# Transposing one more attention output by DMA instead of on TensorE, in a fused attention and MLP kernel

## The chip, the cores and the metric

The kernel runs on one core of one Trainium2 chip. The metric is device time in microseconds (us) of one execution; lower is better.

## The reference

Sliding-window attention with a few global keys and a distance bias, followed by an MLP with squared ReLU. The shapes are batch 4, 8 heads, 768 positions and head size 64; `n_global` is 8 and `n_local` is 96. In the MLP there are 3072 tokens, a model width of 512 and an inner width of 2048.

```python
scores = scale * np.matmul(q, k.transpose(0, 1, 3, 2))
...
keep = is_global | is_local
...
scores = np.where(keep, scores + bias, -1000000000.0)
a = np.exp(scores - np.max(scores, axis=-1, keepdims=True))
a = a / (np.sum(a, axis=-1, keepdims=True) + 1e-09)
x = np.matmul(a, v)                      # then to (tokens, heads * head size)
h = x @ w_in
r = np.maximum(h, 0.0)
out = (r * r) @ w_out
```

## The kernel before

The 3072 tokens are cut into 24 tiles of 128, six for each batch element. The MLP works on blocks of two tiles, so there are 12 blocks. Block 3, which matters here, consists of tiles 6 and 7.

**Attention of one tile j.** GpSimd issues the loads of q, k and v (line 213). From tile 6 on, q and k land in a ring of three slots, so the load of tile j waits until tile j-3 has been read. q and k are transposed into `qkT`. Tiles 0 to 5 do that on TensorE (`tr`, line 402), and the others by one DMA transpose on SyncE's queue (`T`, line 426). TensorE makes the scores of the tile with itself and with its left neighbour (`sc`, line 489, 16 matmuls, or 8 for the first tile of a batch element). These contract over 64 rows only. ScalarE takes the exponential (`exp`, line 555), VectorE multiplies by the bias and mask (`mul`, line 580), TensorE multiplies by v (`pv`, line 642, two groups of 8 matmuls into `po`), and VectorE divides by the row sum into `x` (`norm`, lines 669 and 670).

**From x to the MLP.** The MLP needs x with the model width on the partitions. There are two ways, chosen by `j < JX` in line 698. Tiles below JX are transposed on TensorE by four matmuls with the identity into a PSUM buffer (`trx`, line 705), which ScalarE or VectorE then copies to `xT` (line 332, or 330). The other tiles use one DMA transpose on SyncE's queue (`xT`, line 729), and nothing else. `JX` is 8.

**MLP of one block.** A block has eight steps. `s1` (line 757) is eight matmuls of 256 columns; it needs `xT` of both tiles of its block. ScalarE takes the ReLU (line 778) and VectorE squares it (line 790). `s2` (line 830) is four matmuls of 512 columns into two accumulators. After the eighth step the result is copied out (`o`) and stored from SyncE's queue (`st`, line 872). Up to 14 squared tiles `hs` can wait for their `s2`. In the text below, s1 steps are numbered through: step 24 is the first of block 3.

**Order.** Each engine executes its instructions in one fixed order, written out before the kernel runs. A small planner (class `Plan`) makes it: it gives every operation a duration, a set of operations it depends on and a rank (`key`), and always takes the operation with the smallest start plus 0.01 times its rank. So 100 points of rank stand for 1 us. The tables around the change only move ranks and dependencies. `SHIFT` adds to the rank of a kind of operation, or of that kind in one tile. `LEADS` moves all the attention of a tile ahead of its block's MLP steps. `STEP` names the s1 step after which a tile's scores may come, and `HOLD` makes the following s1 step wait for those scores. A gate (line 376), which is a tiny write on VectorE, delays the loads of tiles 8 to 10, since the load has to come after it.

For a DMA transpose of x the planner counts 1.2 us on SyncE's queue, and 0.9 us of transfer with two lags of 0.6 and 1.2 us; for some tiles more is added by `SAFEX` (tiles 9, 11 and 13). The transposes of q and k have such additions for tiles 6 to 11 and 14 to 16 in `SAFE`.

Of the kernel before, what the change touches and what calls it, by code (L numbers as in the profile page):

```python
# [21 lines left out]
class Plan:  # L22
# [8 lines left out]

    LAG = {"PE": 0.25, "ACT": 0.26, "DVE": 0.2, "SP": 0.6, "POOLQ": 0.8, "DMAQ": 1.2, "DMA": 0.0}
    URGE = 0.01
    SHIFT = {'T': 47, 'sc': -5.25, 'pv': -2, 'norm': 26.5, 'trx': -2, 'xT': 51, 'gk': 42, 'gv': -127.5, 'mul': 24, 'kl': 38.5, 'relu': 25.5, 'sq': 30, 's2': -5, 'o': 61, 'st': 78, ('mul', 3): 28, ('tr', 4): 10, ('xT', 5): -22, ('sc', 6): 14, ('pv', 7): -4, ('norm', 7): -17, ('trx', 7): -3, ('sc', 8): -12, ('pv', 8): -18, ('pv', 10): 45, ('sc', 11): 12, ('pv', 12): -50, ('sc', 13): 17, ('sc', 14): 6, ('pv', 14): 10, ('norm', 14): -28, ('sc', 15): -21, ('exp', 15): 20, ('exp', 16): 83, ('mul', 16): 92, ('norm', 16): -9, ('sc', 17): 32, ('pv', 17): 28, ('pv', 21): 9.5, ('pv', 22): -10, ('norm', 22): 8, ('s1', 2): -8.5, ('sq', 2): -10, ('relu', 3): 24, ('sq', 3): -82, ('s1', 5): 6, ('s1', 6): 30, ('sq', 6): 6, ('s1', 7): -6, ('sq', 7): -92, ('relu', 8): 40, ('s1', 9): -2, ('s1', 10): -10, ('s2', 0): 7.5, ('s2', 2): 1, ('s2', 4): -15, ('s2', 5): 37, ('s2', 6): -5, ('s2', 7): -3, ('s2', 9): 4.5, ('s2', 11): 30}

    def shift(self, name):
        early = name[-1 if name[0] in ("T", "tr") else 1]
        return self.SHIFT.get(name[0], 0.0) + self.SHIFT.get((name[0], early), 0.0)

# [65 lines left out]
def kernel(  # L105
# [35 lines left out]
    NFIRST = 4  # L141
    NSPLIT = 4
    NBIAS = 3
    JQK, JX = 6, 8
    NQ, NKT = 3, 2 * TPB
    NG = 8 - NACC
    G = ("g", NG)
# [7 lines left out]
    def const(shape, dt, name):  # L155
        return consts.tile(shape, dt, name=name, tag=name)
# [18 lines left out]
    pbt = const([P, 2, P], FP32, "pbt")  # L175
    pbw = const([P, 2, P], FP32, "pbw")
    plan = Plan()
    LEADS = {3: 51, 4: 17, 5: 16, 6: 27, 8: 2, 9: 20, 10: 42, 11: 47, 12: 0, 14: 0, 15: 7.5, 16: 34, 17: 46, 20: 28, 21: 15, 23: 56}
    SAFE = {j: 1.6 for j in range(6, 12)} | {14: 4.2, 15: 3.2, 16: 3.5}
    SAFEX = {9: 1.5, 11: 1.5, 13: 2.5}  # L180

# [2 lines left out]
    JOIN = {(7, 0), (12, 0), (21, 0), (16, 0), (23, 0), (18, 0), (20, 0), (15, 0)}  # L184
    COPY = [14, 15, 19, 20, 22]
    BEHIND = {}
    HOLD = ((10, 0),)
    STEP = {(4, 0): -7, (12, 0): 37, (5, 0): -2, (10, 0): 29, (13, 0): 30, (23, 1): 81}
    JGATE = 11
    NHS = 14  # L190
    NWARM = 8
# [12 lines left out]
    def slot(j):  # L204

        return j if j < NFIRST + 2 else NFIRST + 2 + j % NQ
# [57 lines left out]
    def emit_ones(e, js):  # L264
        for j in js:
            nc.vector.memset(v_sb[j][:, :, D : D + 1], 1.0)
# [38 lines left out]
    for g in range(NFIRST + 2, NT, 6):  # L305
        js = range(g, min(g + 6, NT))
        o = plan.op(
            ("ones", g), {"DVE": 0.2}, lambda e, js=js: emit_ones(e, js),
            key=-1.0, ready=15.0,
        )  # L310
# [40 lines left out]
    kl = [const([P, NPAIR, P], BF16, f"kl_{i}") for i in range(2 if COPY else 0)]  # L351
# [8 lines left out]
    for j in range(NT):  # L360
        b, t = divmod(j, TPB)
        first = t == 0
        need = 8 * (j // 2)
        base = need - LEADS.get(j, LEAD) + 4 * (j % 2)
        if (j, 0) in JOIN:
# [3 lines left out]
        if j in late:  # L369
            def emit_load(e, j=j):  # L370
                load_tile(j)
            gate = None
            if NFIRST + 2 + NQ - 1 <= j < JGATE:

                def emit_gate(e, j=j):
                    nc.vector.memset(qk_ring[slot(j)][:, :, :1], 0.0)

                gate = plan.op(
                    ("gate", j), {"DVE": 0.07}, emit_gate, deps=qk_users[slot(j)] + [ld, xT_sp.get(j - 3)],
                    key=base - 9,  # L380
                )
# [13 lines left out]
        for n in range(2) if j < JQK else ():  # L395
            users = []

            def emit_tr(e, j=j, n=n, fp=fp):
# [9 lines left out]
            tr = plan.op(  # L408
                ("tr", n, j), {"PE": 0.5 if fp else 0.24}, emit_tr,
                deps=[land["qk"[n], j]], key=base, takes=(*G, [users]),  # L410
            )
# [12 lines left out]
        if j >= JQK:  # L424
            def emit_dT(e, j=j, T_=T_):
# [5 lines left out]
            T = plan.op(  # L431
                ("T", j), {"SP": 1.3}, emit_dT,
                deps=[land["q", j], land["k", j], xT_op[j - 3]] + ku, key=base - 6,
            )
            T = plan.op(("moved", j), {"DMAQ": 1.2}, None, deps=[T])
            qk_users[slot(j)].append(T)
            if j in SAFE:

                T = plan.op(("seen", j), {"DMA": SAFE[j]}, None, deps=[T])
# [6 lines left out]
        mul, mul_users = {}, {}  # L446
# [55 lines left out]
        for gs in SETS.get(j, [tuple(range(groups))]):  # L502
            n = 8 * len(gs)
            sc_users = busers[2 * gs[0] : 2 * gs[-1] + 2]
            if (j, gs[0]) in JOIN:

                o, also, taken = joint
# [16 lines left out]
            if j < NBIAS:  # L524
# [6 lines left out]
            o = plan.op(  # L531
                ("sc", j, gs[0]), {"PE": 0.2 + 0.029 * n},
                lambda e, gs=also, f=emit_sc: f(e, gs), deps=[*deps, bias],
                key=base + 1 + 2 * gs[0], takes=takes,
            )
# [91 lines left out]
        norm = []  # L627
# [170 lines left out]
    for o in plan.ops:  # L798
        if o["name"][0] == "sc":
            j = o["name"][1]  # L800
            n = STEP.get(o["name"][1:], 4 * j - LEAD)
            if n >= 0 and j >= NFIRST:
                o["deps"].append(s1_ops[n // NSTEP, n % NSTEP])
                if o["name"][1:] in HOLD:
                    n += 1
                    s1_ops[n // NSTEP, n % NSTEP]["deps"].append(o)

    for blk in range(NBLK):
# [9 lines left out]
        for s, sub, half in order2:  # L818
# [5 lines left out]
            def emit_s2(e, blk=blk, s=s, sub=sub, half=half, w=w, cols=cols, own=own):  # L824
# [15 lines left out]
            o = plan.op(  # L840
                ("s2", blk, s, sub), {"PE": 0.43 * w / d_model}, emit_s2,
                deps=[d, land["wout", s]] + users[-1:],
                key=8 * blk + s + 2.0 + (0 if not last else 8 * sub + 8 * (half or 0)),
                takes=((*G, [users]) if own else ("acc", NACC, [users])) if s == 0 else None,
            )
# [6 lines left out]
            if s == NSTEP - 1:  # L852
# [14 lines left out]
                def emit_st(e, blk=blk, sub=sub, half=half, cols=cols):  # L867
# [9 lines left out]
                st = plan.op(  # L877
                    ("st", blk, sub), {"SP": 0.8 if (blk, sub) in HALVES else 0.4}, emit_st,
                    deps=[ev, s1_ops[NLATE, 0] if blk < NLATE - 2 else None],
                    key=8 * blk + s + 9.0,  # L880
                )
                st = plan.op(("stored", blk, sub), {"DMAQ": 1.4}, None, deps=[st])
# [40 lines left out]
```

## Time and profile before

| | before |
|---|---|
| median of 5 runs | 211.81 us (211.33 to 212.38) |
| the profiled execution: its own time | 211.69 us |
| its span in the profile | 209.9 us |
| TensorE matmuls, busy | 202.5 us (96% of the span) |
| VectorE / ScalarE busy | 141.0 us / 120.2 us |
| `trx` transposes on TensorE | 32, four for each of tiles 0 to 7 |
| DMA transposes of x / of q and k | 16 / 18 |

The span is what the profile covers, from the first to the last instruction of the kernel; the execution's own time is 1.8 us longer. "Busy" for matmuls counts overlapping instructions once, and a matmul's recorded duration includes the time in which the next has already started, so the distance between the starts of two matmuls tells more than their durations. A few matmul records are missing from a trace. Of the 400 `s2` matmuls, 373 have one.

### The profile page before, as it was taken

Reading aid. Unit: us, or ns where it says so; the run is one execution under the profiler, and the core shown is the slowest. Engines: PE = TensorE matmul, PEld = TensorE weight load, DVE = VectorE, ACT = ScalarE, POOL = GpSimd, SP = SyncE. Lnnn points to the kernel's source line nnn. Section 1 sums busy time; section 2 is a strip of 40 time slices with the busy share of each in tenths; the row PEclk is TensorE's granted clock in tenths of the full one; section 3 lists DMA queues with packets and bytes.
Section 4 is the critical chain, followed back from the end, with each engine's and each line's share of the span. In section 5 each row is a group of like instructions: output and inputs, shape, how many; then the busy total and the mean of one; then the engine's idle time right before and its main releaser. Section 6 shows DMA issues by size and latency. Waiting matters only on the chain.

```text
span 209.9 us, 4980 instructions
## 1 busy us (share of the span) xinstructions
PE 202.5 (96%) x1957; PEld 141.3 (67%) x1984; DVE 141.0 (67%) x370; ACT 120.2 (57%) x224; POOL 73.9 (35%) x91
## 2 busy tenths in 40 slices
PE   7988999999999999999999999999999999999994
PEld 3766877666756677676866676776676865865853
DVE  7689698533595878585958666676696865781730
ACT  6766678234772674664737464663575826841631
POOL 8996676531568048232455143222500000000000
PEclk9999999999999999999999999999999999999999
DMA  9999999999999999979999994989983421130402
GB/s 128 153 160 185 182 190 200 179 162 142 211 132 163 201 120 158 192 119 134 175 146 108 217 97 58 139 120 144 195 61 75 123 55 28 53 97 3 102 0 100
DMA packets 112649, 27.32 MB, mean 130 GB/s; under 512 B 103282, under 2 KB 109682, under 8 KB 112626
## 3 DMA queue, kind: packets, MB, share of 16 engines
q0 software_dynamic: 79200, 13.37, 83.8%
q1 hardware_dynamic: 33426, 13.64, 35.6%
q8 instruction: 15, 0.25, 0.5%
q14 instruction: 8, 0.07, 0.1%
HBM read 27.26 MB, written 6.29 MB: 160 GB/s over the span
## 4 chain that ended last, share of the span: by engine, by line
PE 88%; POOL 5%; DMA 4%; issue 1%; DVE 1%; ACT 0%; POOLq 0%
PE acc L830 39%; PE hT L757 39%; PE sc L489 5%; PE po L642 4%; DMA win<-in_moe_w_in_dram 4%; POOL qk L213 3%; POOL v L213 2%; POOL win L213 1%; PE trx L705 1%; PE tr L402 1%; DVE x L670 0%; DVE hs L790 0%; POOL pbi L269 0%; DVE rs L669 0%; ACT o L330 0%
## 5 line engine op out<-in xcount | busy, mean ns | idle before, releaser
L757 PE MATMUL hT<-xT,win 128*128 128x256 bf16 x768 | 93.5, 273 | 0.8 <-DMA win<-in_moe_w_in_dram 0.8
L830 PE MATMUL acc<-wout,hs 128*128 128x512 bf16 (+2 forms) x373 | 87.1, 370 | 1.7 <-issue 0.3
L778 ACT ACTIVATE hr<-hT 128x512 f32<-128x512 f32 x96 | 57.4, 603 | 47.4 <-PE hT L757 41.8
L757 PEld LDWEIGHTS <-win 128*128 128x128 bf16 x768 | 72.6, 97 | 15.3 <-DMA win<-in_moe_w_in_dram 1.4
L790 DVE TENSOR_TENSOR hs<-hr 128x512 bf16<-128x512 f32 x96 | 64.7, 686 | 23.2 <-ACT hr L778 22.4
L830 PEld LDWEIGHTS <-hs 128*128 128x128 bf16 x400 | 36.7, 97 | 33.9
L555 ACT ACTIVATE esc<-sc 128x512 bf16<-128x512 f32 x78 | 39.9, 613 | 13.2 <-PE sc L489 13.2
L213 POOL DMA_DIRECT2D qk<-in_q_dram x23 | 20.8, 903 | 69.7 <-DMA qkT<-qk 57.4
L580 DVE TENSOR_TENSOR at<-esc,E 128x512 bf16<-128x512 bf16 x78 | 32.3, 422 | 10.0 <-ACT esc L555 7.2
L330 ACT COPY o<-acc 128x512 f32<-128x512 f32 (+2 forms) x21 | 11.6, 576 | 19.8 <-PE acc L830 19.8
L213 POOL DMA_DIRECT2D v<-in_v_dram x24 | 21.9, 914 | 1.4 <-DMA win<-in_moe_w_in_dram 1.1
L670 DVE TENSOR_TENSOR x<-po,rs 128x256 bf16<-128x256 f32 x48 | 20.4, 424 | 1.7
L213 POOL DMA_DIRECT2D qk<-in_k_dram x23 | 20.7, 902 | 0.6 <-DMA win<-in_moe_w_in_dram 0.5
L642 PEld LDWEIGHTS <-at 128*128 128x128 bf16 x352 | 15.6, 97 | 5.5 <-ACT at L555 0.9
L642 PE MATMUL po<-v,at 128*128 128x65 bf16 x352 | 17.3, 194 | 0.7 <-DMA v<-in_v_dram 0.7
L669 DVE RECIPROCAL rs<-po 128x4 f32<-128x4 f32 x48 | 8.5, 177 | 11.8 <-PE po L642 11.4
L489 PEld LDWEIGHTS <-qkT 64*128 64x128 bf16 x312 | 9.4, 94 | 5.6 <-issue 4.9
L489 PE MATMUL sc<-qkT 64*128 64x128 bf16 x192 | 12.5, 219 | 0.0
L489 PE MATMUL sc<-qkT,qkT 64*128 64x128 bf16 x120 | 8.5, 216 | 0.0
L332 DVE COPY o<-acc 128x512 f32<-128x512 f32 x4 | 2.8, 692 | 6.2 <-PE acc L830 6.2
L213 POOL DMA_DIRECT2D win<-in_moe_w_in_dram x8 | 6.2, 804 | 1.6 <-DMA win<-in_moe_w_in_dram 1.2
L213 POOL DMA_DIRECT2D wout<-in_moe_w_out_dram x8 | 5.7, 718 | 2.3 <-DMA win<-in_moe_w_in_dram 1.6
(45 smaller groups left out, 68.7 us busy)
## 6 DMA issues: line engine op xcount, KB each, us to landing
out_dram<-o SPq DMA_DIRECT2D x21, 256.0 KB, 3.5
v<-in_v_dram POOLq DMA_DIRECT2D x24, 128.0 KB, 5.9
qk<-in_q_dram POOLq DMA_DIRECT2D x23, 128.0 KB, 5.1
qk<-in_k_dram POOLq DMA_DIRECT2D x23, 128.0 KB, 5.4
win<-in_moe_w_in_dram POOLq DMA_DIRECT2D x8, 256.0 KB, 8.3
wout<-in_moe_w_out_dram POOLq DMA_DIRECT2D x8, 256.0 KB, 9.2
out_dram<-o SPq DMA_DIRECT2D x4, 128.0 KB, 2.4
qkT<-qk SPq DMA_TRANSPOSE x18, 5.5
```

The costliest lines, as they stand in the source:

```text
L213: nc.gpsimd.dma_start(out=dst, in_=src)
L330: nc.scalar.copy(dst, src)
L489: nc.tensor.matmul(out=tiles["sc", j, odd, g][:, at, :], lhsT=left[j - 1][half, pair, :] if kt else qkT[j % NKT][half, 1, pair, :], rhs=qk ...
L555: nc.scalar.activation(out=esc, in_=tiles.pop(("sc", j, odd, g)).rearrange("p a c -> p (a c)"), func=Act.Exp, scale=scale,)
L580: nc.vector.tensor_mul(at, tiles.pop(("esc", j, odd, g)), bias)
L642: nc.tensor.matmul(out=po[:, hi, :], lhsT=tiles["at", j, odd, g][:, at * P : (at + 1) * P], rhs=v_sb[kj][:, h, :], start=(i == 0), stop=(i ...
L669: nc.vector.reciprocal(rs, po[:, :, D : D + 1])
L670: nc.vector.tensor_tensor(out=x[:, 4 * hf : 4 * hf + 4, :], in0=po[:, :, :D], in1=rs.to_broadcast([P, 4, D]), op=Alu.mult,)
L757: nc.tensor.matmul(out=hT[:, c, :], lhsT=w_in_sb[s][:, kt, c * P : (c + 1) * P], rhs=tiles["xT", blk][:, kt, :], start=(kt == 0), stop=(kt ...
L778: nc.scalar.activation(hr, tiles.pop(("hT", blk, s)), Act.Relu)
L790: nc.vector.tensor_mul(hs, hr, hr)
L830: nc.tensor.matmul(out=tiles["acc", blk, sub, half], lhsT=hs[:, c, sub * P : (sub + 1) * P], rhs=w_out_sb[s][:, c, cols], start=(s == 0 an ...
```

## The change

`JX` becomes 7. Tile 7 then takes the second way: its four `trx` matmuls and the copy out of PSUM are gone, and one DMA transpose on SyncE's queue is added, with s1 of block 3 waiting for it. The rank tables for tiles 6 to 17 and blocks 3 to 7 are replaced by other values. Entries for tiles 0 to 5 and the general entries stay. Since the gate of tile 10 depends in the plan on the DMA transpose of x of tile 7, where there is one, that gate comes after it.

```diff
-    SHIFT = {..., ('sc', 6): 14, ('pv', 7): -4, ('norm', 7): -17, ('trx', 7): -3, ('sc', 8): -12, ('pv', 8): -18, ('pv', 10): 45, ...}
+    SHIFT = {..., ('T', 6): -28.0, ('sc', 6): 6.0, ('mul', 6): -0.5, ('pv', 6): -20.5, ('norm', 6): 8.5, ('trx', 6): 11.5, ('T', 7): 6.0, ('exp', 7): -2.0, ('gk', 7): 41.0, ('pv', 7): 24.5, ('norm', 7): 1.5, ('xT', 7): 1.0, ('gate', 8): -8.5, ('T', 8): 7.0, ('sc', 8): 3.0, ('exp', 8): -24.0, ('pv', 8): 127.0, ('norm', 8): 5.0, ...}
...
-    JQK, JX = 6, 8
+    JQK, JX = 6, 7
...
-    LEADS = {3: 51, 4: 17, 5: 16, 6: 27, 8: 2, 9: 20, 10: 42, 11: 47, 12: 0, 14: 0, 15: 7.5, 16: 34, ...}
+    LEADS = {3: 51, 4: 17, 5: 16, 6: 49.5, 8: 140.0, 9: 30.0, 10: 27.0, 11: 48.0, 12: 14.0, 14: 0, 15: -25.5, 16: 34, ..., 7: 46.5, 13: 0.0}
...
-    HOLD = ((10, 0),)
-    STEP = {(4, 0): -7, (12, 0): 37, (5, 0): -2, (10, 0): 29, (13, 0): 30, (23, 1): 81}
+    HOLD = ((23, 1),)
+    STEP = {(4, 0): -7, (12, 0): 37, (5, 0): -2, (10, 0): 25, (13, 0): 39, (23, 1): 81, (6, 0): 17, (8, 0): 18, (9, 0): 27, (11, 0): 25, (14, 0): 35, (15, 1): 54}
```

A tile without an entry in `LEADS` has 12 (tile 7 before); a tile without one in `STEP` may have its scores after s1 step 4j - 12 (so step 12 for tile 6, 20 for tile 8, 24 for tile 9 and 32 for tile 11 before). `SAFE`, `SAFEX` and the tables of which scores are issued together are as before.

More of the change, by code (lines that the diff above doesn't have):

```diff
@@ L33 @@
     URGE = 0.01
-    SHIFT = {'T': 47, 'sc': -5.25, 'pv': -2, 'norm': 26.5, 'trx': -2, 'xT': 51, 'gk': 42, 'gv': -127.5, 'mul': 24, 'kl': 38.5, 'relu': 25.5, 'sq': 30, 's2': -5, 'o': 61, 'st': 78, ('mul', 3): 28, ('tr', 4): 10, ('xT', 5): -22, ('sc', 6): 14, ('pv', 7): -4, ('norm', 7): -17, ('trx', 7): -3, ('sc', 8): -12, ('pv', 8): -18, ('pv', 10): 45, ('sc', 11): 12, ('pv', 12): -50, ('sc', 13): 17, ('sc', 14): 6, ('pv', 14): 10, ('norm', 14): -28, ('sc', 15): -21, ('exp', 15): 20, ('exp', 16): 83, ('mul', 16): 92, ('norm', 16): -9, ('sc', 17): 32, ('pv', 17): 28, ('pv', 21): 9.5, ('pv', 22): -10, ('norm', 22): 8, ('s1', 2): -8.5, ('sq', 2): -10, ('relu', 3): 24, ('sq', 3): -82, ('s1', 5): 6, ('s1', 6): 30, ('sq', 6): 6, ('s1', 7): -6, ('sq', 7): -92, ('relu', 8): 40, ('s1', 9): -2, ('s1', 10): -10, ('s2', 0): 7.5, ('s2', 2): 1, ('s2', 4): -15, ('s2', 5): 37, ('s2', 6): -5, ('s2', 7): -3, ('s2', 9): 4.5, ('s2', 11): 30}
+    SHIFT = {'T': 47.0, 'sc': -5.25, 'pv': -2.0, 'norm': 26.5, 'trx': -2.0, 'xT': 51.0, 'gk': 42.0, 'gv': -127.5, 'mul': 24.0, 'kl': 38.5, 'relu': 25.5, 'sq': 30.0, 's2': -5.0, 'o': 61.0, 'st': 78.0, ('mul', 3): 28.0, ('tr', 4): 10.0, ('xT', 5): -22.0, ('T', 6): -28.0, ('sc', 6): 6.0, ('mul', 6): -0.5, ('pv', 6): -20.5, ('norm', 6): 8.5, ('trx', 6): 11.5, ('T', 7): 6.0, ('exp', 7): -2.0, ('gk', 7): 41.0, ('pv', 7): 24.5, ('norm', 7): 1.5, ('xT', 7): 1.0, ('gate', 8): -8.5, ('T', 8): 7.0, ('sc', 8): 3.0, ('exp', 8): -24.0, ('mul', 8): -1.0, ('gk', 8): 1.0, ('pv', 8): 127.0, ('norm', 8): 5.0, ('gv', 8): 4.5, ('xT', 8): -0.5, ('gate', 9): -6.0, ('T', 9): -6.5, ('sc', 9): -6.5, ('exp', 9): 6.0, ('gk', 9): 0.5, ('pv', 9): 5.5, ('norm', 9): 6.0, ('gv', 9): -4.5, ('xT', 9): 8.0, ('T', 10): -12.5, ('sc', 10): 3.0, ('mul', 10): -8.5, ('gk', 10): 1.0, ('pv', 10): -1.0, ('norm', 10): -5.0, ('gv', 10): -3.0, ('xT', 10): -0.5, ('T', 11): 3.5, ('sc', 11): -13.0, ('exp', 11): -10.5, ('mul', 11): -8.0, ('pv', 11): -8.0, ('norm', 11): -3.0, ('xT', 11): -5.5, ('T', 12): 1.5, ('exp', 12): -7.5, ('mul', 12): -13.0, ('pv', 12): -6.0, ('norm', 12): -0.5, ('xT', 12): 0.5, ('T', 13): -6.5, ('sc', 13): -3.0, ('exp', 13): 7.5, ('mul', 13): 0.5, ('gk', 13): -6.5, ('pv', 13): -19.5, ('norm', 13): -2.0, ('gv', 13): 13.0, ('T', 14): -9.0, ('sc', 14): 8.0, ('exp', 14): 11.5, ('mul', 14): -1.5, ('pv', 14): -28.0, ('gv', 14): 0.5, ('xT', 14): -13.5, ('T', 15): -1.5, ('sc', 15): -5.5, ('mul', 15): -11.5, ('kl', 15): -7.0, ('pv', 15): -24.5, ('norm', 15): -9.5, ('gv', 15): 3.0, ('xT', 15): -11.0, ('exp', 16): 83.0, ('mul', 16): 92.0, ('norm', 16): -9.0, ('sc', 17): 32.0, ('pv', 17): 28.0, ('pv', 21): 9.5, ('pv', 22): -10.0, ('norm', 22): 8.0, ('s1', 2): -8.5, ('sq', 2): -10.0, ('s1', 3): -3.5, ('relu', 3): 3.5, ('relu', 4): 11.5, ('sq', 4): 67.5, ('s1', 5): -7.5, ('relu', 5): 4.5, ('sq', 5): -8.0, ('s1', 6): 2.5, ('relu', 6): -6.0, ('sq', 6): 7.5, ('s1', 7): 4.5, ('relu', 7): 8.0, ('sq', 7): -54.0, ('relu', 8): 40.0, ('s1', 9): -2.0, ('s1', 10): -10.0, ('s2', 0): 7.5, ('s2', 2): 1.0, ('s2', 3): -2.0, ('o', 3): 6.0, ('st', 3): -0.5, ('s2', 4): -32.5, ('o', 4): 6.0, ('s2', 5): 18.5, ('o', 5): -15.0, ('st', 5): 19.5, ('s2', 6): 13.5, ('o', 6): -13.0, ('st', 6): -6.0, ('s2', 7): 6.5, ('st', 7): -8.5, ('s2', 9): 4.5, ('s2', 11): 30.0}
@@ L177 @@
     plan = Plan()
-    LEADS = {3: 51, 4: 17, 5: 16, 6: 27, 8: 2, 9: 20, 10: 42, 11: 47, 12: 0, 14: 0, 15: 7.5, 16: 34, 17: 46, 20: 28, 21: 15, 23: 56}
+    LEADS = {3: 51, 4: 17, 5: 16, 6: 49.5, 8: 140.0, 9: 30.0, 10: 27.0, 11: 48.0, 12: 14.0, 14: 0, 15: -25.5, 16: 34, 17: 46, 20: 28, 21: 15, 23: 56, 7: 46.5, 13: 0.0}
     SAFE = {j: 1.6 for j in range(6, 12)} | {14: 4.2, 15: 3.2, 16: 3.5}
```

## The prediction

> **What bounds the kernel now.** I read the page's first lines, then what TensorE waited for, then the order of its matmuls around tile 7, then SyncE's queue. The page says that the matmul row is full, and that the DMA engines are, too, for the first 24 of 40 slices.
>
> ```profile
> span 209.9 us, 4980 instructions
> PE 202.5 (96%) x1957; PEld 141.3 (67%) x1984; DVE 141.0 (67%) x370; ACT 120.2 (57%) x224; POOL 73.9 (35%) x91
> ...
> PE   7988999999999999999999999999999999999994
> ...
> DMA  9999999999999999979999994989983421130402
> ```
>
> A full row of recorded matmuls may still hide gaps, so I went to the waits of TensorE. Columns: engine, line and what it waited for, then us in total, times, longest.
>
> ```profile
> PE warm L275 <- DVE zero L263: 1.2, 1, 1.2
> PE hT L757 <- DMA win<-in_moe_w_in_dram: 0.8, 2, 0.4
> PE po L642 <- DMA v<-in_v_dram: 0.7, 1, 0.7
> PE acc L830 <- issue: 0.3, 2, 0.2
> ```
>
> The first three lie before 20 us, in the part whose tables aren't touched. From 20 to 200 us I took the distances between matmul starts in the timeline: s1 matmuls follow each other every 109 ns, s2 every 216 ns, transposes every 56 ns. Two kinds of larger gap occur. One is a hole of about 0.22 us in the s2 rows, which is a missing record, not a stall (its size is one s2 matmul, and the records fall 27 short). The other stands around each group of scores: 0.10 us before it and 0.12 us after it. **So TensorE's stream has no stall to win back after 20 us**; time goes down only by taking matmuls out, or by having fewer groups of scores.
>
> Next, the matmuls between the transposes of tile 7 and the first s1 step of block 3 (start, duration of the merged row, engine, line, what):
>
> ```profile
> 60.30 0.39 PE L705 MATMUL trx<-ident,x 128*128 128x128 bf16 x4
> ...
> 61.17 2.33 PE L830 MATMUL acc<-wout,hs 128*128 128x512 bf16 x10
> 63.34 0.41 PE L642 MATMUL po<-v,at 128*128 128x65 bf16 x8
> ...
> 64.69 1.89 PE L830 MATMUL acc<-wout,hs 128*128 128x512 bf16 x8
> 66.41 0.27 PE L757 MATMUL hT<-xT,win 128*128 128x256 bf16 x1
> ```
>
> Counting s1 in eights and s2 in fours from the start of the trace, with the missing records put back, gives 24 s1 steps and 24 s2 steps done at 66.41 us. The store of squared tiles is empty. Until then TensorE lived on s2 of block 2, and at 66.41 it has nothing left except s1 of block 3. That step needs x of tile 7 transposed. Last, SyncE's queue, and the landing times of its DMA transposes of x (all 16, and the one nearest to tile 7, issued at 65.59):
>
> ```profile
> 58.79 2.40 SPq L426 DMA_TRANSPOSE qkT<-qk  x1
> 65.59 1.19 SPq L729 DMA_TRANSPOSE xT<-x  x1
> ...
> DMA to landing us min/median/max: 2.4/3.3/6.5
> ...
> DMA to landing us min/median/max: 5.0/5.0/5.0
> ```
>
> **What the Trainium skill says.** (1) "TensorEngine Tiling (Array Packing)", Key Properties: changing the tiling mode drains TensorE. The scores contract over 64 rows, all else over 128; the 0.10 + 0.12 us at each group agree. (2) "DMA: Bandwidth & Descriptors", Issuing engines are not separate DMA queues: transfers of all engines share the same 16 DMA engines. The trace fits: the landing is 5.0 us at 65.6 us, where the DMA row is full, and 2.4 us at 91.8 us (in the table by stretches the DMA share is 2.23 from 65 to 70 us and 0.66 from 90 to 95). (3) The same page, Anatomy of one DMA: about 2.0 us fixed plus bytes over 436 GB/s, fitted for GpSimd's path; for 128 KB an estimate of 2.3 us. The shortest landing here, 2.4 us, agrees; under load the measured ones replace it.
>
> **The change part by part.**
>
> Removed from TensorE: four transposes. In the chain they take 0.22 us (four times 56 ns). TensorE has no slack behind them, so the whole 0.22 us comes off the end. The gap before the scores that follow them (0.10 us) stays with whatever stands there.
>
> Removed from ScalarE: one copy out of PSUM of 585 ns (60.72 us), preceded by 1.11 us of idle time. ScalarE is 57% busy; worth nothing at the end. A PSUM buffer is free about 0.9 us sooner; no wait of TensorE for one is listed, so nothing.
>
> Added on SyncE: one DMA transpose, 1.19 us of its queue by the L729 row. x of tile 7 is ready at 60.08 us (last normalization: 59.66 + 0.42). In the order of before the queue is issuing the q/k transpose of tile 9 from 58.79 to 61.19. The transpose would then be issued at 61.2. Landing: 2.4 us at best, so 63.6; 5.0 us as for the neighbour, so 66.2; 6.5 us at worst, so 67.7. It is needed at 66.41 - 0.22 = 66.2. I take 5.0, because the DMA engines are as full there. So it fits with nothing to spare in the old order; the new ranks give some. Tile 7 gets 34.5 points (LEADS 12 to 46.5), and net of SHIFT its second-to-last steps gain 6 points (pv) and 16 (norm), that is 0.06 to 0.16 us of rank; tile 6, which goes ahead of it, gains 22.5. I value that at 0 to 1 us earlier, since the scores of tile 7 start at 53.2 us and the shortest chain from there is six exponentials at about 0.6 us, a multiplication (0.42), pv (0.24) and two normalizations (0.6 each), about 5.6 us, so 58.8 rather than 60.08. Expected stall: 0, range 0 to 1.5 us.
>
> Behind it on SyncE: the transpose of tile 8's x (its data ready at 65.5), two stores and the q/k transpose of tile 10 (67.98). The first stands idle from 61.2 to 65.59 waiting for its data, so the added 1.19 us fit there. If the new one goes ahead of tile 9's instead, tile 9 lands some 1.2 us later than its roughly 65.4 (a load that waits for it starts at 65.65); its scores start at 69.13. Nothing.
>
> Added to the DMA engines: 128 KB. At least 0.33 us (at 400 GB/s, which single slices reach), at most the 2.4 us of the shortest landing. Loads behind it slip by that. The next thing late is the q/k transpose of tile 10: it waits for its load, lands at 75.4 (67.98 + 7.4), and its scores start at 76.36, a margin of 0.96 us. The gate of tile 10 (61.66 us, load at 62.02) also comes after the added transpose now; at an issue by 61.2 that costs nothing. A slip of 0 to 1.5 us past the margin is thus possible if the scores stay where they are; tile 10 belongs to block 5, whose s1 begins at 97.9, so an order that puts them later loses nothing. I take 0.
>
> Moved: the ranks of tiles 6 to 17. Loads, q/k transposes, stores, exponentials and normalizations change places on GpSimd, SyncE, ScalarE and VectorE as well as on TensorE; the number of each is unchanged. Their cover is TensorE's stream, and its value is between -0.44 us (two of the ten groups of scores from 41 to 154 us come next to another one, 0.22 us each; STEP lets tiles 10 and 11 both come from step 25, tiles 6 and 8 from 17 and 18) and an unknown stall where an operand lands later than its place. Two groups more cost +0.44. I take 0. Tiles 18 to 23 keep their tables.
>
> Sum: 211.69 - 0.22 + 0 = 211.47 us against the profiled execution (span 209.9 to 209.7). That execution lies 0.12 below the median, so 211.59 against the median of 211.81.
>
> **The rivals.** A measurement of this kernel can tell about 0.3% (0.64 us) from no change.
>
> *Likeliest, no measurable change:* -0.22, with one or two groups of scores merged or split and a stall under 0.85. Its own range is 211.2 to 212.4. For: the stall-free stream and the backlog that just covers the transfer. Chance 0.50.
>
> *Slower:* the landing of tile 7's x replaces the copy as what block 3 waits for. Place: first s1 of block 3, with no s2 left to run. Price: each us that it lands after 66.2 is a us of TensorE, and nothing gives it back, because the stream after it has no idle time. At the worst landing seen (6.5) it is 1.5 us: 211.81 - 0.22 + 1.5 = 213.1. It decides from a landing 0.86 us too late. For: the planner counts 0.9 + 1.2 + 0.6 us after the 1.2 of the queue, 3.9 us from issue, where the neighbour's trace has 5.0 and SAFEX has no entry for tile 7; and a static order over some ten tiles holds more such places (tile 10's scores, margin 0.96). Against: x of tile 7 can be ready over a us sooner. Chance 0.41.
>
> *Faster beyond 0.3%:* two groups of scores merge: -0.22 - 0.44 = -0.66, so 211.15. Against: each operand of such a pair must have landed, and tile 8's lands at 58.0 (issued 52.53, 5.5 us), five us after tiles 6 and 7 start. Chance 0.09.
>
> *The change does not do what it says:* excluded by the branch in line 698, which has no other condition.
>
> **How the numbers follow.** 211.6 is the likeliest case. The range 211.2 to 213.6 takes in that case and most of the slower one (213.1, with half a us for a second late operand); about 0.07 is left below it and 0.12 above.
>
> **What would show it.** L705 with 28 matmuls, L729 with 17 transposes, one copy L330 or L332 of xT fewer; TensorE's busy time down by 0.2. A wait of PE or PEld at L757 for the DMA of xT near 66 us would show the slower rival, with its size; one at L489 for a q/k transpose would show the second place. Fewer than ten score groups between 41 and 154 us would show the faster one. The prediction is wrong if the time falls by over 0.64 us, since I find nothing to pay for that, or if a stall stands where all transposes have landed early.

## The result, and the profile after

| | before | after |
|---|---|---|
| median of all executions in the comparison | 211.63 us (46 runs, 211.0 to 214.67) | 213.59 us (27 runs, 211.55 to 216.48) |
| ratio after / before | | 1.0063, 95% interval 1.0043 to 1.0082 |
| profiled execution: time, span | 211.69, 209.9 us | 212.43, 210.7 us |

The change makes the kernel slower, by 0.4 to 0.8% in this comparison and by 0.2 to 0.5% in three later ones (the smallest of these is not clear of no change). The ratio is of the fast executions alone: it leaves out those more than 1.5% above the fastest of their kernel, one of before and six of after, and since five of these six ran at a granted clock of 0.999 or 1.0, long stalls may be among what it leaves out. The spread tells as much as the middle: the runs of after reach from 211.6, where they equal the kernel before, to over 216.

The page of the kernel after, its first lines, as they were shown of before:

```profile
span 210.7 us, 4978 instructions
PE 202.6 (96%) x1956; PEld 141.1 (67%) x1980; DVE 140.7 (67%) x368; ACT 121.2 (58%) x225; POOL 73.9 (35%) x91
...
PE   7997999999999999999999999999999999999993
...
DMA  9999999999999999997999979999993331220402
```

Nothing in it but the span shows a loss; busy time of matmuls is as good as unchanged although four were removed (376 of the `s2` matmuls have a record here, 373 before). The edit itself is there. The answer of the trace for tile `trx` gives 28 matmuls, where before had 32:

```profile
L705 PE MATMUL trx<-ident,x x28: 218/219/229, 10.9 to 58.3; 128*128 128x128 bf16 x28
```

The answer for the line of the DMA transposes of x gives 17 of them, where before had 16:

```profile
L729 SPq DMA_TRANSPOSE xT<-x x17: 1188/1192/1651, 59.5 to 185.0; - x17
```

The waits of TensorE, after (waiting line, what it waited for, us in total, times, longest):

```profile
PE hT L757 <- DMA win<-in_moe_w_in_dram: 1.5, 2, 1.0
PE warm L275 <- DVE zero L263: 1.2, 1, 1.2
PE sc L489 <- DMA qkT<-qk: 0.4, 1, 0.4
PE acc L830 <- DVE qkT L616: 0.3, 2, 0.2
```

One line is new past the start: scores wait for a DMA transpose of q and k. The timeline of TensorE says which (start, duration of the merged row, what; idle time before it in brackets):

```profile
64.91 1.04 PE L757 MATMUL hT<-xT,win 128*128 128x256 bf16 x8
...
75.23 2.79 PE L757 MATMUL hT<-xT,win 128*128 128x256 bf16 x24
78.45 0.23 PE L489 MATMUL sc<-qkT 64*128 64x128 bf16 x2 [0.44 <-DMA qkT<-qk]
```

s1 step 24, which needs tile 7's x, starts at 64.91 without a wait. The scores of **tile 10**, at 78.45, do wait. SyncE's queue in the timeline of after, ahead of these scores (start, duration, what):

```profile
59.55 1.20 SPq L729 DMA_TRANSPOSE xT<-x  x1
60.85 1.62 SPq L426 DMA_TRANSPOSE qkT<-qk  x1
67.61 1.19 SPq L729 DMA_TRANSPOSE xT<-x  x1
68.89 1.01 SPq L872 DMA_DIRECT2D out_dram<-o  x2
70.00 5.45 SPq L426 DMA_TRANSPOSE qkT<-qk  x2
```

The added transpose (59.55) stands ahead of tile 9's (60.85; it was issued at 58.79 before). Tile 10's is issued at 70.00 instead of 67.98, and takes 8.4 us to land instead of 7.4.

**Two tables that carry the rest.** Both are worked out from the starts in the trace. The first cuts the execution at s1 steps. Within a stage the same order takes the same time to 0.01 or 0.03 us in all profiles, unless something waits, so a stall shows as a number.

| us | start to s1 step 16 | step 16 to 24 to 32, together | 32 to 48 | 48 to 64 | 64 to the start of the last matmul | step 16 to the start of the last matmul | from there to the end of the span |
|---|---|---|---|---|---|---|---|
| before | 41.98 | 38.89 | 31.00 | 33.91 | 61.08 | 164.88 | 3.04 |
| after | 42.04 | 40.92 | 30.13 | 32.18 | 61.94 | 165.17 | 3.45 |

The first column, whose order on TensorE the change does not touch, lay anywhere from 41.05 to 42.81 in the profiles of this study (42.60 in a second one of before). It is left out of all that follows. The stall-free time of the new order from step 16 is 164.65 us (profile `t10_first` below). Against 164.88 that is the 0.22 us of the four transposes, to 0.01.

**The last column** is the same in every profile of a kernel, and it separates the kernels in two. The four that have 64 DMAs issued by SyncE (before, `null_before`, `less_load_before` and `pe7_new_order` below) take 3.03 to 3.05 us there. The twelve profiles of kernels with the added transpose, 65 DMAs, take 3.44 to 3.48. So one more DMA costs 0.42 us after the last matmul. How SyncE ends the kernel, first before, then `load_only` (the kernel before plus one transpose that nobody reads): its last two stores (line 872), what its closing waits (line 918) waited for, and the instructions that follow these waits:

```profile
L872 SPq DMA_DIRECT2D out_dram<-o x2: 333/336/338, 206.7 to 207.4; - x2
SPq L918 <- DMA out_dram<-o: 0.7, 2, 0.4
L918 SPq DRAIN x3: 7/7/13, 209.1 to 209.4; - x3
```

```profile
L872 SPq DMA_DIRECT2D out_dram<-o x2: 333/336/338, 207.1 to 207.7; - x2
SPq L918 <- DMA out_dram<-o: 1.2, 1, 1.2
L918 SPq DRAIN x3: 7/7/7, 209.8 to 210.1; - x3
```

At the end SyncE makes nine waits in a fixed order, each for semaphores (counters on which DMAs and engines report that they are done). The DMAs of SyncE report on eight semaphores in turn. With 64 of them the last store reports on the last of the eight, number 118, and with 65 on the first, number 101. It lands 1.6 us after its issue in both. But 118 belongs to the ninth wait, and 101 to the second: the seven waits behind that one, which have nothing left to wait for, then follow 0.06 us apart. This is read from the traces; no run changes the number of SyncE's DMAs in any other way.

The second table is the room of an operand: start of its first use on TensorE minus the landing of its DMA transpose, in us. 0.04 or 0.05 is the least that occurs, and means that the use came right behind the landing. (The second profile of before is `null_before`.)

| operand, first use | before, two profiles | after | after, 2nd, 3rd, 4th profile |
|---|---|---|---|
| x of tile 7, s1 step 24 | (no DMA) | 0.50 | 0.05, 1.61, 0.65 |
| q/k of tile 10, its scores | 0.94, 1.65 | 0.05 | 0.33, 0.05, 0.05 |
| q/k of tile 13, its scores | 5.01, 2.67 | 0.05 | 0.09, 0.05, 0.05 |
| x of tile 15, s1 step 56 | 2.25, 3.16 | 0.33 | 0.26, 0.25, 0.49 |
| x of tile 17, s1 step 64 | 1.79, 0.60 | 0.51 | 2.09, 1.02, 0.05 |

The new order has five places with hardly any room. Which of them stalls changes from one execution to the next. In the four profiles of after the stalls past step 16 add up to 0.52, 0.43, 1.73 and 0.85 us (time from step 16 minus 164.65), 0.88 in the mean. Less the 0.22 gained and with the 0.42 at the end, that is +1.08 us or 0.51%, beside ratios of 1.0063, 1.0023, 1.0050 and 1.0048 in the four comparisons. Without any stall the change would still cost 0.20 us, or 0.1%.

### The profile page after: what moved, and what is told of

It is laid out like the page before. It is cut to its first block, busy times and chain, and to the rows that moved or that the text cites. A ratio compares the mean times of both kernels' runs of the same rounds, so it can differ in the third digit from the quotient of the medians.

```text
span 210.7 us, 4978 instructions
## 1 busy us (share of the span) xinstructions
PE 202.6 (96%) x1956; PEld 141.1 (67%) x1980; DVE 140.7 (67%) x368; ACT 121.2 (58%) x225; POOL 73.9 (35%) x91
## 4 chain that ended last, share of the span: by engine, by line
PE 84%; DMA 8%; POOL 5%; issue 1%; ACT 0%; SPq 0%; DVE 0%; POOLq 0%
PE acc L830 37%; PE hT L757 37%; PE sc L489 4%; PE po L642 4%; DMA qkT<-qk 4%; DMA win<-in_moe_w_in_dram 4%; POOL qk L213 3%; POOL v L213 2%; POOL win L213 1%; PE tr L402 1%; PE trx L705 0%; ACT hr L778 0%; POOL pbi L269 0%; ACT o L330 0%; SPq L872 0%
## 5 line engine op out<-in xcount | busy, mean ns | idle before, releaser
L830 PE MATMUL acc<-wout,hs 128*128 128x512 bf16 (+2 forms) x376 | 88.1, 370 | 1.4 <-DVE qkT L616 0.3
L330 ACT COPY o<-acc 128x512 f32<-128x512 f32 (+2 forms) x23 | 12.8, 573 | 18.8 <-PE acc L830 18.6
L616 DVE COPY qkT<-qkT 128x32 bf16<-128x32 bf16 x11 | 3.1, 281 | 5.4 <-PE sc L489 5.4
```

The source lines that it names most:

```text
L330: nc.scalar.copy(dst, src)
L830: nc.tensor.matmul(out=tiles["acc", blk, sub, half], lhsT=hs[:, c, sub * P : (sub + 1) * P], rhs=w_out_sb[s][:, c, cols], start=(s == 0 an ...
```

## The experiments

All kernels below keep the planner's result and move single entries of the emitted order, since a new entry in its tables moves everything after it. The helper takes the order out of `plan.run`, moves an operation before or after another, or shifts all the operations of one kind and tile in time.

```diff
-    for o in plan.run({...}):
+    for o in reorder(plan.run({...}), moves, shifts):
```

Each group ran on one chip with its own runs of the kernel before. Ratios are to before, with their 95% interval.

### First group: order or transfer?

**after_again**, the changed kernel itself.

> The changed kernel as it is, for a second profile and as the base of the other runs on the same chip. Order theory (the scores of tile 10 stand at a place in TensorE's stream where the q/k transpose of tile 10 has not landed, because SyncE issues it behind the transpose of tile 8's x): again a wait of TensorE at the scores of tile 10 near 78 us, of 0.3 to 2.5 us, and 212.4 to 214. Landing theory (the first s1 of block 3 waits for the DMA transpose of tile 7's x): a wait at L757 near 65 us in this profile, which the first profile did not have, and the same time.

1.0023 (0.9999 to 1.0046); the median, 211.73 us, lies below what both theories expected. This profile had a wait that the first one had not, in the list of TensorE's matmul waits:

```profile
PE hT L757 <- DMA xT<-x: 0.3, 1, 0.3
```

The list of the weight loads' waits has the same place, and the scores beside it:

```profile
PEld L757 <- DMA xT<-x: 0.7, 1, 0.7
PEld L489 <- DMA qkT<-qk: 0.4, 1, 0.4
```

Here it was tile 7's x that came late, at 64.29 for a use at 64.34. So neither theory holds alone.

**dma7_old_order**: the order before, with only the transposes of tile 7 exchanged.

```diff
-  ("trx", 7): four nc.tensor.transpose;  ("xT", 7): copy out of PSUM
+  ("trx", 7): nothing;  ("xT", 7): nc.sync.dma_start_transpose(...)   # ahead of ("T", 9) on SyncE
```

> The kernel before, with its order on all engines, in which only the four TensorE transposes and the copy of tile 7's x are replaced by one DMA transpose on SyncE, ahead of tile 9's q/k transpose. Order theory: 211.2 to 211.8, that is 0.2 less than before, or no gain where the 0.96 us margin of tile 10's scores is used up. Landing theory: slower, since s2 runs out at 66.2 us here as well: 212.4 to 213.6, with a wait at L757.

1.0021 (1.0006 to 1.0036). Slower where 0.1% of gain had been possible. Its profile shows no large wait after step 16: 164.78 us, and tile 7's x had 2.02 us of room. Against before that is 0.10 us less, and the end of the kernel takes 0.42 us more: +0.32 us or 0.15%, within the interval. Tile 9's transpose went out 3.6 us later here than in before (62.39), and in this profile nothing stalled for it.

**t10_first**: the new order with tile 10's q/k transpose ahead of tile 8's x.

```diff
+ moves = [(("T", 10), "before", ("xT", 8))]
```

> The changed kernel, with SyncE issuing the q/k transpose of tile 10 ahead of the transpose of tile 8's x and of the two stores after it; nothing else moves. Order theory: tile 10 lands 2 to 3 us earlier (75 to 76.5 us), the wait at its scores is gone, 211.3 to 212.0. Landing theory: unchanged, 212.4 to 214.

1.0018 (1.0000 to 1.0037). Tile 10 landed at 71.35 and had 6.45 us of room; the profile had no stall past step 16 (164.65 us). With the end of the kernel that is +0.19 us, or 0.1%. The median, 211.74 us, is what the order theory forecast, but after_again had 211.73 on the same chip. So the wait at tile 10 is real; whether taking it away alone brings the mean time down, these runs cannot tell.

**pe7_new_order**: the new order, with tile 7's x back on TensorE.

```diff
+ moves = [(("xT", 7), "after", ("s2", 2, 2, 1))]
-  nc.sync.dma_start_transpose(out=xT, in_=x)              # tile 7
+  four nc.tensor.transpose into PSUM; nc.scalar.copy(xT, trx)
```

> The changed kernel with its new order, in which tile 7's x is again transposed by four TensorE matmuls and a ScalarE copy (placed after the s2 matmuls near 60.8 us); one DMA transpose fewer. Order theory: the wait at tile 10's scores stays (its transpose is issued as late), 212.6 to 214.2, 0.2 more than the changed kernel. Landing theory, or the load of the added DMA on the others: cured, 211.6 to 212.2.

0.9991 (0.9974 to 1.0008). This is 0.3% less than after_again on the same chip, although TensorE has 0.22 us more to do. So the new order without the added transfer costs nothing that can be seen in the mean, and the order theory fails. The end of the kernel accounts for 0.2 of the 0.3%, the four transposes for 0.1 the other way; the 0.2% left for landings is not clear of the noise by itself. Nor is this order free of stalls. In this profile x of tile 17 had 0.04 us of room at s1 step 64:

```profile
144.82 1.38 PE L757 MATMUL hT<-xT,win 128*128 128x256 bf16 x11 [0.39 <-DMA xT<-x]
```

What the added transfer did to tiles 10 and 13 shows in SyncE's queue:

```profile
57.70 1.32 SPq L426 DMA_TRANSPOSE qkT<-qk  x1
67.13 1.19 SPq L729 DMA_TRANSPOSE xT<-x  x1
```

Tile 9's transpose goes out at 57.70 us, not at 60.85. Its data were there. In after it stands behind tile 7's x, which has to wait for the normalization until 59.5. Tile 12's load needs tile 9's slot: it starts at 65.82 here, and at 67.56, 66.81, 68.69 and 67.58 in the four profiles of after. It then runs beside tile 10's transpose. Tile 10 had 1.32 us of room here and tile 13 had 1.23.

### Second group: more room, and load alone

**after_third**, the base.

> The changed kernel again, as the base on this chip; its ratio to the kernel before was 1.0063 in the first comparison and 1.0023 in the second, so 212 to 213.5. Landing theory (three operands land within 0.1 to 0.7 us of the place where TensorE wants them: tile 7's x at s1 step 24, the q/k of tile 10 and of tile 13 at their scores): a wait at one or more of these three in the profile. Load theory (the added 128 KB make all transfers later, wherever they are used): waits elsewhere too.

1.0050 (1.0021 to 1.0079). The largest stall of the study, in its timeline of TensorE:

```profile
76.00 2.78 PE L757 MATMUL hT<-xT,win 128*128 128x256 bf16 x24
80.39 0.23 PE L489 MATMUL sc<-qkT 64*128 64x128 bf16 x2 [1.61 <-DMA qkT<-qk]
```

Tile 10's transpose took 9.5 us to land (70.80 to 80.34). The matmul stream is the same; the same gap was 0.44 us in the first profile.

**s1_later**: s1 step 24 behind the two pv groups of tile 8 and the last s2 of block 2.

```diff
+ shifts = [("s1", (3, 0), 1.9), ("relu", (3, 0), 1.9), ("sq", (3, 0), 0.4)]
```

> The changed kernel with s1 step 24 placed 1.35 us later in TensorE's stream, behind the two pv groups of tile 8 and the last s2 of block 2 (its ReLU and square move with it); all else in place. Landing theory with tile 7's x as the main cost: 0.4 to 1 us less than the changed kernel on this chip, down to 211.2 to 211.6. If the scores of tiles 10 and 13 are the main cost, or the load: no change against the changed kernel.

1.0043 (1.0021 to 1.0064), no clear gain. Tile 7's x got 1.26 us of room. In this profile it was tile 15 that stalled: 0.05 us of room at s1 step 56, and 0.7 us of waiting. The scores of tile 10 had 0.05 us as well.

**all_three**: that, t10_first, and all of tile 13 later by two s2 groups.

```diff
+ moves = [(("T", 10), "before", ("xT", 8))]
+ shifts = [... as above ..., (k, (13,), 1.3) for k in ("sc", "exp", "mul", "gk", "pv", "norm", "gv", "xT")]
```

> The changed kernel with more room at all three places: s1 step 24 later by 1.35 us, tile 10's q/k transpose issued ahead of tile 8's x transpose, the scores and all the rest of tile 13 later by 0.86 us. Landing theory: no wait for a DMA transpose after 40 us, and below the kernel before by the 0.2 us of the removed matmuls: 211.0 to 211.4, ratio 0.998 to 1.000. Load theory: still 0.2 to 0.6% above the kernel before.

1.0049 (1.0028 to 1.0070): the landing theory of three places fails, and the ratio is what the load theory forecast. The three places had 2.42, 6.00 and 5.06 us of room, as intended, and x of tiles 15 and 17 both came to 0.05. From step 16 it took 165.69 us. The three edits also cost something themselves: stage 40 to 48, with no late transfer in it, took 13.97 instead of 13.72 us.

**load_only**: before, plus one transpose of tile 7's x that nobody reads.

```diff
   ("xT", 7): copy out of PSUM
+  nc.sync.dma_start_transpose(out=junk7, in_=x)
```

> The kernel before, unchanged in its order and its TensorE transposes, with one more DMA transpose of tile 7's x, issued ahead of tile 9's q/k transpose, into a buffer that nothing reads. It adds the load and the time on SyncE's queue, and takes nothing away. Landing theory: same as before, ratio 0.999 to 1.001, since before has 0.9 us or more of room at its tightest later place. Load theory: 0.2 to 0.6% slower.

1.0018 (0.9998 to 1.0038). Stage by stage the profile equals before up to the last matmul (164.88 us), although tile 9's transpose went out at 62.70 us. The end of the kernel takes 0.42 us more, which is 0.2% and the whole of the ratio's excess. The interval just holds 1; the load theory, which looked for later transfers that cost time, gets no support from this profile.

### Third group: who goes first on SyncE

**null_before**, before against itself.

> The kernel before, unchanged, entered as if it were a new one: what does the comparison show where nothing differs? Every theory expects a ratio of 1.000 with an interval that holds it. If it comes out 0.1 to 0.2% high, then so much of the excess of the other kernels (all of them ran 0.5 us later than before ahead of the first touched instruction in some profiles) belongs to the start of the execution and not to the edits.

0.9998 (0.9981 to 1.0015). The comparison shows no bias beyond 0.2%; single ratios of 1.002 are no larger than that, and count here only where a profile shows where the time goes.

**t9_first**: the new order, tile 9's q/k transpose ahead of tile 7's x.

```diff
+ moves = [(("xT", 7), "after", ("T", 9))]
```

> The changed kernel, with SyncE issuing the q/k transpose of tile 9 ahead of the DMA transpose of tile 7's x; nothing else moves. Blocking theory (tile 7's x transpose waits at the head of SyncE's queue until 59.5 us and holds back tile 9's by about 3 us; with it the load of tile 12, which needs tile 9's slot and then runs beside tile 10's transpose): tile 9 is issued near 57.7 instead of 60.9, the load of tile 12 starts near 65.8 instead of 67.6, tile 10 lands by 76.5 instead of 77 to 80, the waits at the scores of tiles 10 and 13 are gone or under 0.2 us, tile 7's x lands as before; ratio to before 0.999 to 1.002. Theory that the new order is too tight by itself: the waits stay, 1.003 to 1.006.

1.0062 (1.0039 to 1.0084). The first half came as expected: tile 9 issued at 57.73, tile 10 with 3.88 us of room, tile 13 with 4.30. The second half did not. SyncE's queue, and the landing of the transpose of x issued at 59.17, with who waited for it:

```profile
57.73 1.33 SPq L426 DMA_TRANSPOSE qkT<-qk  x1
59.17 10.33 SPq L729 DMA_TRANSPOSE xT<-x  x2
```

```profile
  PE hT L757: 1.1, 1
...
DMA to landing us min/median/max: 6.4/6.4/6.4
```

Tile 7's x was issued as early as in after, but it landed after 6.4 us, behind tile 9's 256 KB, instead of 4.9, and s1 step 24 waited 1.1 us for it. The x of tile 15 had 0.05 us of room as well. (Five executions stand behind this ratio.)

**dma7_old_t9**: the same exchange in the old order.

> The kernel before with its order, in which tile 7's x is transposed by DMA, issued behind tile 9's q/k transpose instead of ahead of it; four TensorE transposes and a copy fewer. Blocking theory: tile 9 issued near 58.8 as in the kernel before; tile 7's x issued near 61.2, landing 65 to 66.5, needed at 66.2, so a wait of 0 to 0.5 us in some executions; from s1 step 16 to the end 164.66 us plus that wait, against 164.88 before; ratio 0.999 to 1.001. Landing theory: a wait of 0.5 to 1.5 us at s1 step 24, ratio 1.002 to 1.006.

```diff
   dma7_old_order
+ moves = [(("xT", 7), "after", ("T", 9))]
```

1.0033 (1.0019 to 1.0047). Tile 9 issued at 58.11; tile 7's x issued at 59.72, landed at 66.29 (6.6 us), used at 66.33. The waits of TensorE:

```profile
PE hT L757 <- DMA xT<-x: 0.7, 1, 0.7
```

This is the prediction's rival to the letter: no s2 is left, and step 24 waits for the landing. The landing theory's forecast for this run came true, the blocking theory's did not. Stage 16 to 24 took 25.03 us against 24.22 in dma7_old_order.

### Fourth group: less for the DMA engines to do

Curing one place had moved the stall to another. The question left was whether late landings are the cause as a whole, or something else in the order.

**after_fourth**, the base.

> The changed kernel, as the base on this chip. All theories: 1.002 to 1.006 of the kernel before, with a wait in the profile at one or more of five places where a DMA transpose lands within half a us of its use: s1 step 24 (x of tile 7), the scores of tiles 10 and 13, s1 step 56 (x of tile 15) and s1 step 64 (x of tile 17).

1.0048 (1.0027 to 1.0070), with waits at two other places again:

```profile
PE hT L757 <- DMA xT<-x: 0.3, 1, 0.3
PE sc L489 <- DMA qkT<-qk: 0.3, 1, 0.3
```

These are tile 13's scores (96.11) and s1 step 64 (145.88).

**less_load_after** and **less_load_before**:

```diff
-  nc.gpsimd.dma_start(out=v_sb[j], in_=v)     # tiles 8 to 17
+  nc.gpsimd.memset(v_sb[j], 0.5)
```

> The changed kernel with less for the DMA engines to do: the ten loads of v for tiles 8 to 17 are left out, and GpSimd fills those buffers with 0.5 instead, so the output is not the reference's. All orders and matmuls are as in the changed kernel. Landing theory (the change loses because transfers land too late for the new order): the transposes land 1 to 3 us earlier, the five margins grow above 0.5 us, no wait after 41 us, 164.65 us from s1 step 16 to the last matmul, ratio 0.998 to 1.000. If something in the order other than transfers costs the time: still 1.002 to 1.006.

> The kernel before with the same ten loads of v left out and filled by GpSimd, as the control (output again not the reference's). It has no wait for these transfers, so nothing to gain: 164.88 us from s1 step 16 to the last matmul, ratio 0.999 to 1.001 by every theory; if it gains as much as the changed kernel does, then less load helps for another reason, such as the start.

less_load_after: 1.0018 (0.9998 to 1.0037), where after_fourth has 1.0048 on the same chip. Tile 10 had 3.62 us of room, tile 13 had 4.04, and the x of tiles 7, 15 and 17 had 0.57, 0.55 and 2.10. From step 16 it took 164.89 us, not the 164.65 that was expected: one wait was left, at a place outside the five. The scores of tile 7 came right behind the landing of its q and k (52.50 us), and the weight loads' waits have it:

```profile
PEld L489 <- DMA qkT<-qk: 0.2, 1, 0.2
```

less_load_before: 1.0001 (0.9986 to 1.0017) and 164.88 us from step 16. So less load gives the changed kernel 0.3%, just clear of the noise, and the kernel before nothing, with all orders unchanged. The profiles of the pair give the same: 165.50 minus 164.89, 0.61 us or 0.29%. That is what late landings predict. The 0.18% that remain above before are what the removed matmuls (-0.22 us), the wait at tile 7's scores (0.24) and the end of the kernel (0.42) come to: 0.44 us or 0.21%. The edit also shortens GpSimd's own work (569 ns for a fill, 914 for the issue of a load), so that less traffic and earlier loads are not told apart; both act through landings.

## Why the prediction was wrong

It forecast no measurable change at 0.50 and the slower side at 0.41. The measured median lies at the upper end of its range, on the side that was not chosen. Three of its terms that were put at nothing failed, and a fourth it did not have at all.

*Held.* TensorE has no stall to win back after 20 us: from step 16 to the last matmul the new order, free of stalls, differs from the old one by the four transposes alone, 0.22 us as summed. There are ten groups of scores between 41 and 154 us in both, so nothing was won or lost there. And TensorE never gave a stall back: the stages after one have their usual length. The gain beyond 0.3% was rightly called nearly impossible.

*Failed: "the whole 0.22 us comes off the end".* The sum ends with TensorE's stream, and no term of it looks at what SyncE does after the last matmul. The added transfer costs 0.42 us there, in all twelve profiles that have it and in none of the four that do not. So the likeliest case was +0.20 us and not -0.22, before any stall. The profile before shows the closing waits; what one more DMA does to them was not visible in it.

*Failed: the added transpose on SyncE.* The sum had "Behind it on SyncE ... Nothing" for going ahead of tile 9's transpose, from its own 1.19 us and the room of tile 9's scores. The term is not 1.2 us of issue. SyncE issued nothing else while the transpose waited for its data, so the whole wait counts, 57.7 to 60.85, about 3.1 us. And the thing to look at was not tile 9's scores (3.68 us of room in after) but who waits for tile 9's slot: tile 12's load starts 1 to 3 us later and shares the DMA engines with tile 10's transpose. The profile before had shown this chain, with GpSimd's load at 65.65 released by a transpose. In the old order the same delay of tile 9 met enough room and cost nothing up to the last matmul (`dma7_old_order`, `load_only`).

*Failed: "A slip of 0 to 1.5 us past the margin is thus possible ... I take 0".* The place was named, with its 0.96 us, and the slower outcome came from there in the first profile. Zero was taken because an order can put the scores later. The new tables allow them from step 25 and the order has them after step 31; the room there was 0.05 to 0.33 us in four profiles.

*Failed: "Moved ... I take 0".* "An unknown stall where an operand lands later than its place" was the main term: 0.88 us in the mean of four profiles. The new order took room from tile 13's scores (5.01 and 2.67 to 0.05) and from tile 15's x (2.25 and 3.16 to 0.33). Tile 17's x was tight at times in the kernel before too (1.79 and 0.60), so its stalls are not shown to come from the change. That several places would shrink in an order packed for the planner's fixed 3.9 us was to be feared: past step 16, in the four profiles of after, x transposes took 2.4 to 6.9 us to land, those of q and k 3.1 to 10.4.

*The rival was right in kind and too narrow in place.* A landing that TensorE waits for, with no idle time after it, is most of what makes the kernel slower. The rival put it at tile 7's x alone. In the changed kernel that was one place of five (a wait in one of its four profiles); it became the main one where tile 9 goes first, in t9_first and dma7_old_t9, with 1.1 and 0.7 us. The landing of 5.0 us assumed for it was good: 4.9 in the first profile.

*What stays open.* How the 0.88 us divides between the added transfer and the new ranks is not settled. Without the transfer the mean of the new order equals before, yet its one profile has a stall of 0.39 us.

## What to carry to other kernels

When one engine is full from end to end, a change that takes 0.2 us off it is worth 0.2 us at most, and its risk is the sum over all places where an operand lands shortly before its use: list the room of each operand before and after, not only of the one that is moved, and in more than one profile. Here a transfer put into SyncE's queue cost those behind it its whole wait for data, and then whatever waited for their buffers. Of two transfers with close deadlines only one could be first, and the other came too late; look whether either can afford to be second before trading compute for a transfer. And compare what follows the last matmul: here one DMA more cost 0.42 us there, nearly twice what the four transposes had taken.

## What the runs showed that was not expected

The same transpose in the same place of the same order varies by a microsecond or more from one execution to the next: tile 10's in the changed kernel took 8.4, 7.5, 9.5 and 7.8 us in the four profiles. Matmul stages of the same order agree to some 0.03 us. For tile 7's x and tile 9's q/k, issued next to each other, the place in the queue decided: tile 7's x landed after 3.8 to 5.7 us ahead of tile 9's q/k, and after 6.4 and 6.6 behind it. The time from the last matmul to the end, the same to 0.03 us whatever stalled before, changes by 0.42 us with the number of DMAs that SyncE has issued.
